# Two fused feed-forward layers behind a pooled attention on one core: a different byte offset for each token tile's streams, and 32 bytes for the second layer's weights

## The chip, the cores and the metric

One core of one Trainium2 chip runs the whole program. The metric is the device time of one execution in microseconds (us), the median of the runs shown; lower is better.

## The reference

The input x has 12,480 tokens of 128 channels. A pooled attention with 32 inducing rows comes first, and then two feed-forward layers of width 2048, each without a bias:

```python
h = mab(I, x); x = mab(x, h)              # softmax attention, scale 1/sqrt(128)
h = x @ w_in;  g = maximum(0.01 * h, h);  x = g @ w_out       # first layer
h = x @ w_in2; g = h / (1 + exp(-1.702 * h)); x = g @ w_out2  # second layer
```

## The kernel before

The tokens are cut into 25 token tiles: tiles 0 to 22 have 512 tokens, tiles 23 and 24 have 352. After a prologue that loads x, pools it and converts the weights (which arrive in a wider format), all work is a list of steps `(l, t, f)`: layer l, tile t, and one of NF = 16 blocks of 128 hidden units. The program is written out in that order by hand, so every engine's queue has the order of the code.

- `ffn_in` (L774 for the first layer, L778 to L780 for the second) multiplies a block of the input matrix with the tile's tokens into a PSUM bank `h_ps`. In the first layer this is one matmul, of `hw` (the pooled rows times the input matrix) with `at`, the attention weights of the tile. In the second it is three, because both operands are split into an upper and a lower part: `w2h` with `x2h`, `w2l` with `x2h`, `w2h` with `x2l`.
- `ffn_act` applies the nonlinearity on ScalarE (L788; L794 and L795) and writes the upper part `ghi`; VectorE writes the lower part `glo` (L789; L796).
- `ffn_out` (L806 to L808) adds three matmuls into the bank `acc`, of the output matrix `v1` or `v2` with `ghi`, `ghi` and `glo`. It runs LOOK = 3 steps behind `ffn_in`. The last block of a first-layer tile adds a matmul of `lin` with `at` (L810).

A step of the first layer so has four matmuls and one of the second has six. In each, the *stationary* operand is a 128x128 block of a weight matrix, which its own LDWEIGHTS brings in; the *stream* is the token side (`at`, `x2h`, `x2l`, `ghi`, `glo`), 512 or 352 columns of 4 bytes in each partition. All are of the type float32r.

The streams lie in the pool `main`: three buffers of `at`, five each of `ghi` and `glo`, two each of `x2h` and `x2l`, 2048 bytes per partition each. `at` of tiles 2 to 24 is filled by four DMAs of 64 KB on SyncE's queue (`stack`, L662), set ten steps before the tile's first step; `x2h` and `x2l` are filled by `halves` (ScalarE, and VectorE at L515), ten steps before the tile's first step in the second layer.

In the program's address map every weight block of both layers (`hw`, `v1`, `lin`, `w2h`, `w2l`, `v2`) begins 416 bytes past a multiple of 512, and every stream 480 bytes past one. The tiles named `gap` and `gap2` hold nothing; they push the tiles behind them to these positions. Since all sizes of these operands are multiples of 512 bytes, each stream begins 64 bytes behind its stationary operand, counted modulo 512. Below, this difference is called the *relation* of a matmul. One other float32r matmul has another relation: `linear_product` (L732) streams 256 columns of `v1` (at 416) against `hwT` (at 480), relation 448.

Of the kernel before, what the change touches and what calls it, by code (L numbers as in the profile page):

```python
# [10 lines left out]
F32 = mybir.dt.float32  # L11
F32R = mybir.dt.float32r
# [6 lines left out]
P = 128  # L19
LOOK = 3  # L20
# [37 lines left out]
def kernel(  # L58
# [14 lines left out]
    m = inducing.shape[0]  # L73
    DFF = moe_w_in.shape[1]
    NF = DFF // P
    TOK = TC * P
    NT = 2 + (N - 2 * TC * ENDS) // TOK
    assert N == 2 * TC * ENDS + (NT - 2) * TOK
    ch = [P] * (NT - 2) + [ENDS] * 2
    tok = [TC * k for k in ch]  # L80

    col = [TC * ENDS + TOK * t for t in range(NT - 2)] + [0, N - TC * ENDS]
    SCALE = 1.0 / math.sqrt(C)
    NQ = P // m
    NB = TOK // B
    PSUM = bass.MemoryType.PSUM

    const = ctx.enter_context(tc.tile_pool(name="const", bufs=1))
    slots = ctx.enter_context(tc.tile_pool(name="slots", bufs=1))
    wts = ctx.enter_context(tc.tile_pool(name="wts", bufs=1))  # L90
# [4 lines left out]

    mid = (NT - 2) * TOK
    x_mid = x[0, :mid].rearrange("(p j) c -> p j c", p=P)
# [77 lines left out]

    def matrix_in(src, name, tag):

        hi, lo = (wts.tile([P, DFF], F32R, name=f"{name}{h}", tag=f"{tag}{h}") for h in "hl")
        parts = []
        for o in range(0, DFF, CW):  # L180
            c = slice(o, o + CW)
            parts.append((src[:, c].bitcast(U32), hi[:, c], lo[:, c]))
        return (hi, lo), parts

    def matrix_out(src, name):

        w = wts.tile([P, NF, 2, C], F32R, name=name)
        parts = []
# [4 lines left out]
        return w, parts  # L193


    w1 = wts.tile([P, DFF], F32, name="w1", tag="wh")
    w1_parts = [
        (moe_w_in[:, o : o + CW].bitcast(U32), w1[:, o : o + CW], None)
        for o in range(0, DFF, CW)
# [62 lines left out]
    l = xnp.tile([P, NP], F32, name="l")  # L262
# [7 lines left out]
    def slot(t, dtype, name):  # L270
        return slots.tile([P, TOK], dtype, tag=f"slot{t}", name=f"{name}{t}")

# [231 lines left out]
    main = ctx.enter_context(tc.tile_pool(name="main", bufs=2))  # L504
    ps_a = ctx.enter_context(tc.tile_pool(name="ps_a", bufs=2, space=PSUM))


    main.tile([P, 112], F32, tag="gap", name="gap", bufs=1)

    def halves(src, name, pool=const, tag=None):  # L510
        shape = list(src.shape)
        hi = pool.tile(shape, F32R, name=f"{name}h", tag=f"{tag or name}h")
        lo = pool.tile(shape, F32R, name=f"{name}l", tag=f"{tag or name}l")
        nc.scalar.activation(out=hi, in_=src, func=AF.Copy)
        nc.vector.tensor_tensor(out=lo, in0=src, in1=hi.bitcast(F32), op=ALU.subtract)  # L515
        return hi, lo


    at_t = {}

    def weights_tile():


        return main.tile([P, TOK], F32R, tag="at", name="at", bufs=3)

    def token_tile(t, rest):

        st = {}
        n = ch[t]
        bc = lambda v: v.rearrange("p (j u) -> p j u", u=1).to_broadcast([n, TC, m])  # L530
        tiny = lambda name: main.tile([P, TC], F32, tag=name, name=name, bufs=2)[:n]

        def s0():
            ps = ps_h.tile([P, 512], F32, tag="h", name="s2_ps")
            for k in range(TC):
                nc.tensor.matmul(
                    ps[:n, k * m : (k + 1) * m], xT[t][:, k * n : (k + 1) * n],
                    hT[:, 0, :], start=True, stop=True,
                )
            st["ps"] = ps  # L540

        def s0b():
            ps = st["ps"]
            sv = ps[:n, : TC * m].rearrange("p (j k) -> p j k", j=TC)
            mxt = tiny("nmx")
            nc.vector.tensor_reduce(out=mxt, in_=sv, axis=AX.X, op=ALU.max)
            a = main.tile([P, TC, m], F32, tag="na", name="na", bufs=2)[:n]
            nc.vector.tensor_tensor(out=a, in0=sv, in1=bc(mxt), op=ALU.subtract)
            nc.scalar.activation(out=a, in_=a, func=AF.Exp, scale=SCALE)
            st["a"] = a  # L550

        def s1():
            a = st["a"]
            sst = tiny("nsum")
            nc.vector.tensor_reduce(out=sst, in_=a, axis=AX.X, op=ALU.add)
            nc.vector.tensor_scalar_add(sst, sst, EPS)
            nc.vector.reciprocal(sst, sst)
            nc.vector.tensor_tensor(out=a, in0=a, in1=bc(sst), op=ALU.mult)

        def s2():  # L560
            a = st["a"]
            rows = main.tile([P, TC, NQ, m], F32R, tag="rows", name="rows", bufs=2)[:n]
            dup = lambda v: v.rearrange("p j (u k) -> p j u k", u=1).to_broadcast(
                [n, TC, 2, m]
            )
            hi, lo = rows[:, :, 0:NQ:2, :], rows[:, :, 1:NQ:2, :]
            nc.vector.tensor_copy(hi, dup(a))
            rest.tensor_tensor(out=lo, in0=dup(a), in1=hi.bitcast(F32), op=ALU.subtract)
            st["rows"] = rows

        def s3():
            ps = ps_h.tile([P, 512], F32, tag="h", name="rows_ps")
            for k in range(TC):
                nc.tensor.transpose(
                    ps[:, k * n : (k + 1) * n],
                    st["rows"][:, k].rearrange("p q k -> p (q k)").bitcast(F32),
                    ident[:n, :n],
                )
            at_t[t] = weights_tile()[:, : tok[t]]
            nc.scalar.activation(out=at_t[t], in_=ps[:, : tok[t]], func=AF.Copy)  # L580

        return [s0, s0b, s1, s2, s3]

    NG = (NT - 2 + NQ - 1) // NQ
    hl = [None] * NG
# [71 lines left out]

    def stack(t):
        g, q = divmod(t - 2, NQ)
        a = weights_tile()[:, : tok[t]]  # L660
        for k in range(NQ):
            nc.sync.dma_start(  # L662
                out=a[k * m : (k + 1) * m, :].bitcast(F32),
                in_=hl[g][k % 2][q * m : (q + 1) * m, : tok[t]],
            )
        at_t[t] = a
# [62 lines left out]
    def linear_product(b):  # L729
        for k in range(4):  # L730
# [3 lines left out]
                v1[:, f].rearrange("p h c -> p (h c)"),  # L734
                start=(f == 0), stop=(f == NF - 1),
            )
# [25 lines left out]
    x2_t = {}  # L762
    x2h_t = {}
# [18 lines left out]

    def ffn_act(l, t, f):
        o = h_t.pop((l, t, f))
        hi = main.tile([P, TOK], F32R, tag="ghi", name="ghi", bufs=LOOK + 2)[:, : tok[t]]
        lo = main.tile([P, TOK], F32R, tag="glo", name="glo", bufs=LOOK + 2)[:, : tok[t]]
        if l == 0:
            nc.scalar.activation(out=hi, in_=o, func=AF.Relu)  # L788
            nc.vector.scalar_tensor_tensor(  # L789
                out=lo, in0=o, scalar=0.0, in1=hi.bitcast(F32), op0=ALU.max, op1=ALU.subtract  # L790
            )
        else:
            g = main.tile([P, TOK], F32, tag="g", name="g")[:, : tok[t]]
            nc.scalar.activation(out=g, in_=o, func=AF.Silu, scale=BETA)  # L794
            nc.scalar.activation(out=hi, in_=g, func=AF.Copy)  # L795
            nc.vector.tensor_tensor(out=lo, in0=g, in1=hi.bitcast(F32), op=ALU.subtract)  # L796
        g_t[l, t, f] = (hi, lo)

    def ffn_out(l, t, f):
# [4 lines left out]
        v = v1 if l == 0 else late["v2"]  # L804
        end = l == 1 and f == NF - 1
        nc.tensor.matmul(o, v[:, f, 0, :], hi, start=(f == 0), stop=False)  # L806
        nc.tensor.matmul(o, v[:, f, 1, :], hi, start=False, stop=False)  # L807
        nc.tensor.matmul(o, v[:, f, 0, :], lo, start=False, stop=end)  # L808
        if l == 0 and f == NF - 1:
            nc.tensor.matmul(o, lin, at_t.pop(t), start=False, stop=True)  # L810
# [23 lines left out]

    steps = [(l, t, f) for l in range(2) for t in range(NT) for f in range(NF)]
    steps[: 2 * NF] = [(0, t, 4 * b + f) for b in range(NF // 4) for t in (0, 1) for f in range(4)]

# [7 lines left out]
    first = token_tile(0, nc.vector)  # L845
# [41 lines left out]
    for t in range(2, NT):  # L887
        at((t - 1) * NF + (10 if t == 2 else 6), stack, t)

    def late_matrix(make, src, name, args, first):  # L890
# [8 lines left out]
        at(first, begin)  # L899

    late_matrix(matrix_in, moe2_w_in, "w2", ["w"], 60)
    late_matrix(matrix_out, moe2_w_out, "v2", [], 160)

    gaps = []

    def split_x2(t):

        if not gaps:
            gaps.append(main.tile([P, 96], F32, tag="gap2", name="gap2", bufs=1))
        x2h_t[t] = halves(x2_t.pop(t), "x2", main)  # L910

    for t in range(NT):
        at(NT * NF + (t - 1) * NF + 6, split_x2, t)

    for n in range(len(steps) + LOOK):
        if n < len(steps):
            ffn_in(*steps[n])
            ffn_act(*steps[n])
        if n >= LOOK:
            l, t, f = steps[n - LOOK]  # L920
            ffn_out(l, t, f)
            if f == NF - 1:
                ffn_end(l, t)
        for stage in extra.pop(n, []):
            stage()
# [39 lines left out]
```

## Time and profile before

| | |
|---|---|
| median of 2 runs | 964.12 us (963.95 to 964.28) |
| the profiled execution: span from first to last instruction | 962.6 us |
| TensorE (PE) busy | 953.7 us, 99% of the span |
| weight loads (PEld) busy | 779.5 us, 81% |
| ScalarE (ACT) busy | 783.0 us, 81% |
| VectorE (DVE) busy | 631.5 us, 66% |
| GpSimd (POOL) busy | 52.8 us, 5% |

The span stands 1.5 us under the median of the runs; that much lies around it. A matmul's own duration is longer than the distance to the next one's start, since matmuls overlap in the pipeline. What a matmul costs is therefore read as the distance between starts, and the busy share of PE says only that it has no gaps.

### The profile page before, as it was taken

The numbers are of one execution on the slowest core, as the hardware profiler recorded it, in microseconds if no ns is written. First come the engines' busy times: TensorE is split into PE (matmuls) and PEld (weight loads), VectorE is DVE, ScalarE is ACT, GpSimd is POOL, SyncE is SP. The second block draws the span as 40 slices with busy tenths as digits, with TensorE's granted clock in tenths as the row PEclk, the third lists the DMA queues.
The fourth block names the chain that finished last, engine by engine and source line by source line (L and its number), as shares of the span: only waits on it lengthen the run. The fifth ranks groups of instructions, "written<-read, shape, count | busy, mean of one in ns | idle before, by whom it ended". The sixth has DMA issues, their size and how long they took to land.

```text
span 962.6 us, 13196 instructions
## 1 busy us (share of the span) xinstructions
PE 953.7 (99%) x4577; PEld 779.5 (81%) x4577; DVE 631.5 (66%) x1002; ACT 783.0 (81%) x1357; POOL 52.8 (5%) x64
## 2 busy tenths in 40 slices
PE   8999999999999999999999999999999999999998
PEld 6677787887878878898888888888888888888888
DVE  3897788878878777765555555555555555555554
ACT  6666777767767666689999999999999999999998
POOL 1330101102100010000000000000000000000000
PEclk9999999999999999999999999999999999999999
DMA  9302120021000000000000000000000000000000
GB/s 337 107 1 55 34 66 23 20 81 33 23 22 12 23 12 19 8 1 12 12 12 12 12 11 12 15 19 12 12 11 12 12 12 12 12 12 23 12 12 16
DMA packets 15334, 27.90 MB, mean 29 GB/s; under 512 B 2347, under 2 KB 6987, under 8 KB 15267
## 3 DMA queue, kind: packets, MB, share of 16 engines
q1 hardware_dynamic: 15123, 26.88, 9.0%
q8 instruction: 36, 0.59, 0.3%
q14 instruction: 31, 0.25, 0.1%
q10 hardware_dynamic: 144, 0.18, 0.1%
HBM read 14.79 MB, written 6.39 MB: 22 GB/s over the span
## 4 chain that ended last, share of the span: by engine, by line
PE 94%; DVE 3%; DMA 1%; ACT 1%; issue 0%; POOL 0%; SPq 0%; ACTq 0%; POOLq 0%
PE acc L806 18%; PE acc L808 18%; PE acc L807 18%; PE h_ps L778 9%; PE h_ps L780 9%; PE h_ps L779 9%; PE h_ps L774 9%; DVE glo L789 1%; DMA xn<-in_x_dram 1%; PE s_ps L609 1%; PE xT_ps L279 1%; PE acc L810 1%; PE pv_ps L348 0%; DVE v L158 0%; DVE v L153 0%
## 5 line engine op out<-in xcount | busy, mean ns | idle before, releaser
L796 DVE TENSOR_TENSOR glo<-g,ghi 128x512 fp32r<-128x512 f32 (+1 forms) x400 | 271.7, 679 | 236.8 <-ACT ghi L795 223.2
L788 ACT ACTIVATE ghi<-h_ps 128x512 fp32r<-128x512 f32 (+1 forms) x400 | 232.2, 587 | 97.8 <-PE h_ps L774 96.2
L806 PE MATMUL acc<-ghi,v 128*128 128x512 f32 (+1 forms) x800 | 309.8, 387 | 0.0
L789 DVE SCALAR_TENSOR_TENSOR glo<-h_ps,ghi 128x512 fp32r<-128x512 f32 (+1 forms) x400 | 264.4, 674 | 68.8 <-ACT ghi L788 63.8
L808 PE MATMUL acc<-glo,v 128*128 128x512 f32 (+1 forms) x800 | 309.2, 386 | 0.1
L807 PE MATMUL acc<-ghi,v 128*128 128x512 f32 (+1 forms) x800 | 307.5, 384 | 0.0
L794 ACT ACTIVATE g<-h_ps 128x512 f32<-128x512 f32 (+1 forms) x400 | 234.3, 586 | 33.7 <-PE h_ps L780 0.6
L795 ACT ACTIVATE ghi<-g 128x512 fp32r<-128x512 f32 (+1 forms) x400 | 248.4, 621 | 12.7
L808 PEld LDWEIGHTS acc<-glo,v 128*128 128x128 f32 x800 | 150.2, 188 | 32.2 <-DVE glo L789 0.6
L807 PEld LDWEIGHTS acc<-ghi,v 128*128 128x128 f32 x800 | 150.2, 188 | 30.5
L806 PEld LDWEIGHTS acc<-ghi,v 128*128 128x128 f32 x800 | 150.3, 188 | 28.6 <-issue 0.2
L774 PE MATMUL h_ps<-at,hw 128*128 128x512 f32 (+1 forms) x400 | 155.7, 390 | 0.0
L778 PE MATMUL h_ps<-x2h,w2h 128*128 128x512 f32 (+1 forms) x400 | 155.3, 388 | 0.0
L780 PE MATMUL h_ps<-x2l,w2h 128*128 128x512 f32 (+1 forms) x400 | 154.5, 386 | 0.0
L779 PE MATMUL h_ps<-x2h,w2l 128*128 128x512 f32 (+1 forms) x400 | 153.1, 383 | 0.0
L774 PEld LDWEIGHTS h_ps<-at,hw 128*128 128x128 f32 x400 | 75.1, 188 | 18.8 <-issue 3.8
L780 PEld LDWEIGHTS h_ps<-x2l,w2h 128*128 128x128 f32 x400 | 75.1, 188 | 16.2
L779 PEld LDWEIGHTS h_ps<-x2h,w2l 128*128 128x128 f32 x400 | 75.1, 188 | 15.5
L778 PEld LDWEIGHTS h_ps<-x2h,w2h 128*128 128x128 f32 x400 | 75.2, 188 | 13.8
L824 ACT ACTIVATE x<-acc 128x512 f32<-128x512 f32 (+1 forms) x25 | 14.7, 587 | 7.6 <-PE acc L810 7.6
L515 DVE TENSOR_TENSOR x2l<-x,x2h 128x512 fp32r<-128x512 f32 (+1 forms) x25 | 16.8, 672 | 0.0
L283 ACT ACTIVATE xT<-xT_ps 128x512 f32<-128x512 f32 (+1 forms) x25 | 12.7, 586 | 4.6 <-PE xT_ps L279 4.6
(111 smaller groups left out, 312.7 us busy)
## 6 DMA issues: line engine op xcount, KB each, us to landing
out_dram<-o_t SPq DMA_DIRECT2D x23, 256.0 KB, 2.0
xn<-in_x_dram SPq DMA_DIRECT2D x11, 512.0 KB, 9.3
raw<-in_moe_w_in_dram SPq DMA_DIRECT2D x8, 512.0 KB, 5.3
raw<-in_moe_w_out_dram SPq DMA_DIRECT2D x8, 512.0 KB, 4.8
at<-hlhi SPq DMA_DIRECT2D x42, 64.0 KB, 2.0
at<-hllo SPq DMA_DIRECT2D x42, 64.0 KB, 2.0
xn<-in_x_dram SPq DMA_DIRECT2D x1, 352.0 KB
xn<-in_x_dram SPq DMA_DIRECT2D x1, 256.0 KB, 12.4
```

The lines of the kernel that those rows point to most:

```text
L774: nc.tensor.matmul(o, hw[:, cols], at_t[t], start=True, stop=True)
L778: nc.tensor.matmul(o, wh[:, cols], hi, start=True, stop=False)
L779: nc.tensor.matmul(o, wl[:, cols], hi, start=False, stop=False)
L780: nc.tensor.matmul(o, wh[:, cols], lo, start=False, stop=True)
L788: nc.scalar.activation(out=hi, in_=o, func=AF.Relu)
L789: nc.vector.scalar_tensor_tensor(out=lo, in0=o, scalar=0.0, in1=hi.bitcast(F32), op0=ALU.max, op1=ALU.subtract)
L794: nc.scalar.activation(out=g, in_=o, func=AF.Silu, scale=BETA)
L795: nc.scalar.activation(out=hi, in_=g, func=AF.Copy)
L796: nc.vector.tensor_tensor(out=lo, in0=g, in1=hi.bitcast(F32), op=ALU.subtract)
L806: nc.tensor.matmul(o, v[:, f, 0, :], hi, start=(f == 0), stop=False)
L807: nc.tensor.matmul(o, v[:, f, 1, :], hi, start=False, stop=False)
L808: nc.tensor.matmul(o, v[:, f, 0, :], lo, start=False, stop=end)
```

## The change

Each stream buffer gets 512 bytes of room (LINE = 128 elements), and a token tile lays its stream at an offset of its own in it. `place(l, t)` gives the offset in elements: 0 for the two tiles of 352 and for tile 0 (in the first layer tile 1 too, in the second tile 22 too); else 32, 64, ... 512 bytes for sixteen tiles in order, and then 4, 8, 16, 24 and 48 bytes for five more. In the first layer the list begins at tile 2, in the second at tile 1. The second layer's matrices `w2h`, `w2l` and, behind them, `v2` lie 32 bytes later, at 448; the gap is shortened by 32 bytes, so that a stream with offset 0 stays at 480. No instruction is added, taken away or moved in its queue. In the address map after the change, the relation of tile t is 32 + 32 t modulo 512 in both layers for tiles 2 to 16.

```
+    LINE = 128
+    SHIFT = 8
...
-        hi, lo = (wts.tile([P, DFF], F32R, name=f"{name}{h}", tag=f"{tag}{h}") for h in "hl")
+        hi = wts.tile([P, DFF + LINE], F32R, name=f"{name}h", tag=f"{tag}h")[:, SHIFT : SHIFT + DFF]
+        lo = wts.tile([P, DFF + SHIFT], F32R, name=f"{name}l", tag=f"{tag}l")[:, SHIFT:]
...
-    w1 = wts.tile([P, DFF], F32, name="w1", tag="wh")
+    w1 = wts.tile([P, DFF + LINE], F32, name="w1", tag="wh")[:, :DFF]
...
-    main.tile([P, 112], F32, tag="gap", name="gap", bufs=1)
+    main.tile([P, 104], F32, tag="gap", name="gap", bufs=1)
+
+    PLACES = [8 * k for k in range(1, 17)] + [1, 2, 4, 6, 12]
+
+    def place(l, t):
+        first = 2 if l == 0 else 1
+        return PLACES[t - first] if first <= t < first + len(PLACES) and t < NT - 2 else 0
+
+    def stream(name, bufs, l, t):
+        o = place(l, t)
+        return main.tile([P, TOK + LINE], F32R, tag=name, name=name, bufs=bufs)[:, o : o + tok[t]]
...
+    def halves(src, t):
+        hi = stream("x2h", 2, 1, t)
+        lo = stream("x2l", 2, 1, t)
...
+    def weights_tile(t):
+        return stream("at", 3, 0, t)
...
-        hi = main.tile([P, TOK], F32R, tag="ghi", name="ghi", bufs=LOOK + 2)[:, : tok[t]]
-        lo = main.tile([P, TOK], F32R, tag="glo", name="glo", bufs=LOOK + 2)[:, : tok[t]]
+        hi = stream("ghi", LOOK + 2, l, t)
+        lo = stream("glo", LOOK + 2, l, t)
```

## Rows read from the trace of the kernel before

**Rows 1.** The page: shares of the span by engine, and the chain that ended last.
```profile
PE 953.7 (99%) x4577; PEld 779.5 (81%) x4577; DVE 631.5 (66%) x1002; ACT 783.0 (81%) x1357; POOL 52.8 (5%) x64
...
PE 94%; DVE 3%; DMA 1%; ACT 1%; issue 0%; POOL 0%; SPq 0%; ACTq 0%; POOLq 0%
PE acc L806 18%; PE acc L808 18%; PE acc L807 18%; PE h_ps L778 9%; PE h_ps L780 9%; PE h_ps L779 9%; PE h_ps L774 9%; DVE glo L789 1%; DMA xn<-in_x_dram 1%; PE s_ps L609 1%; PE xT_ps L279 1%; PE acc L810 1%; PE pv_ps L348 0%; DVE v L158 0%; DVE v L153 0%
```

**Rows 2.** Busy time by stretch: first layer, second layer, 352-token tiles of the second.
```profile
core 0: us, PE busy (x) PEld busy (x) DVE busy (x) ACT busy (x) POOL busy (x), PEclk, DMA share, GB/s
305.00:340.00 35.00, 35.00 (x155) 28.71 (x154) 26.86 (x41) 23.57 (x40) 0.00 (x0) 1.00 0.10 23
500.00:600.00 100.00, 100.00 (x438) 82.06 (x437) 55.20 (x82) 90.79 (x150) 0.00 (x0) 1.00 0.03 11
926.00:956.00 30.00, 30.00 (x185) 29.60 (x184) 17.50 (x34) 28.47 (x63) 0.00 (x0) 1.00 0.05 16
```

**Rows 3.** One line's instructions, L774, 305 to 340 us: durations, first and last start.
```profile
L774 PE MATMUL h_ps<-at,hw x38: 388/392/394, 305.3 to 339.7; 128*128 128x512 f32 x38
```

**Rows 4.** The same view of L778, 500 to 600 us, then from 926 us on.
```profile
L778 PEld LDWEIGHTS h_ps<-x2h,w2h x73: 188/188/188, 500.0 to 598.9; 128*128 128x128 f32 x73
L778 PE MATMUL h_ps<-x2h,w2h x73: 394/394/394, 500.2 to 599.1; 128*128 128x512 f32 x73
...
L778 PE MATMUL h_ps<-x2h,w2h x32: 321/321/324, 926.0 to 956.4; 128*128 128x352 f32 x32
```

**Rows 5.** Timeline of PE near 59 and 37 us (start, us, what); one matmul's duration.
```profile
59.34 0.63 PE L732 MATMUL lin_ps<-v,hwT 128*128 128x256 f32 x4
...
L732 PE MATMUL lin_ps<-v,hwT x16: 280/281/682, 59.3 to 73.6; 128*128 128x256 f32 x16
...
36.90 0.60 PE L118 MATMUL idle_ps<-idle 128*128 128x256 bf16 x4
...
L118 PE MATMUL idle_ps<-idle x19: 272/421/421, 1.2 to 5.7; 128*128 128x256 bf16 x19
```

**Rows 6.** Groups of instructions by line, 500 to 600 us, then 305 to 340 us.
```profile
L796 DVE TENSOR_TENSOR glo<-g,ghi 128x512 fp32r<-128x512 f32 x74 | 51.3, 693 | 45.3 <-ACT ghi L795 42.6 <-PE h_ps L780 2.3
L795 ACT ACTIVATE ghi<-g 128x512 fp32r<-128x512 f32 x73 | 46.1, 632 | 2.3
L794 ACT ACTIVATE g<-h_ps 128x512 f32<-128x512 f32 x73 | 43.6, 597 | 6.8
...
L789 DVE SCALAR_TENSOR_TENSOR glo<-h_ps,ghi 128x512 fp32r<-128x512 f32 x39 | 26.7, 690 | 8.4 <-ACT ghi L788 8.4
L788 ACT ACTIVATE ghi<-h_ps 128x512 fp32r<-128x512 f32 x38 | 22.7, 599 | 10.9 <-PE h_ps L774 10.8
```

**Rows 7.** Line L662, the DMAs that fill `at`: issues, and time to landing.
```profile
L662 SPq DMA_DIRECT2D at<-hlhi x46: 507/578/1926, 75.5 to 389.0; - x46
L662 SPq DMA_DIRECT2D at<-hllo x46: 507/589/1612, 76.2 to 389.6; - x46
...
DMA to landing us min/median/max: 1.8/2.0/4.8
```

More of the change, by code (lines that the diff above doesn't have):

```diff
@@ L505 @@
     ps_a = ctx.enter_context(tc.tile_pool(name="ps_a", bufs=2, space=PSUM))
-    main.tile([P, 112], F32, tag="gap", name="gap", bufs=1)
[L510 to L513, printed above, removed]
+    main.tile([P, 104], F32, tag="gap", name="gap", bufs=1)
[9 more added lines that the diff above has]
+        lo = stream("x2l", 2, 1, t)
         nc.scalar.activation(out=hi, in_=src, func=AF.Copy)
@@ L519 @@
     at_t = {}
-    def weights_tile():
-        return main.tile([P, TOK], F32R, tag="at", name="at", bufs=3)
+    def weights_tile(t):
+        return stream("at", 3, 0, t)
     def token_tile(t, rest):
@@ L578, in s3 @@
                 )
-            at_t[t] = weights_tile()[:, : tok[t]]
+            at_t[t] = weights_tile(t)
             nc.scalar.activation(out=at_t[t], in_=ps[:, : tok[t]], func=AF.Copy)
@@ L659, in stack @@
         g, q = divmod(t - 2, NQ)
-        a = weights_tile()[:, : tok[t]]
+        a = weights_tile(t)
         for k in range(NQ):
@@ L909, in split_x2 @@
             gaps.append(main.tile([P, 96], F32, tag="gap2", name="gap2", bufs=1))
-        x2h_t[t] = halves(x2_t.pop(t), "x2", main)
+        x2h_t[t] = halves(x2_t.pop(t), t)
     for t in range(NT):
```

## The prediction

> **What bounds the kernel now.** I read the page's shares and the chain that ended last first: TensorE is busy 99% of the span, and 94% of the chain is its matmuls, nearly all of them the seven lines of the two layers [rows 1]. So time can come or go only where one matmul follows the next. [...]
>
> [...] In the second layer 73 starts of L778 lie between 500.2 and 599.1 us: 72 steps of six matmuls, 432 in 98.9 us, or 228.9 ns each [rows 4]. In the first layer 38 starts of L774 lie between 305.3 and 339.7 us: 37 steps of four matmuls and two of L810, 150 in 34.4 us, or 229 ns [rows 3]. The two layers differ in what ACT and DVE do meanwhile and in which buffers they read, and the distance is the same. The 352-column tiles: 31 steps of six from 926.0 to 956.4 us, of which nine matmuls (three steps of the tile before) are still 512 wide; (30.4 - 9 x 0.2289) / 177 gives 160.1 ns [rows 4]. Between the two widths a column costs (228.9 - 160.1) / 160 = 0.43 ns.
>
> **The change part by part.** Nothing is removed, added or moved in a queue; only addresses change. Their prices:
>
> *Streams at another relation.* The streams of 21 tiles in each layer move: 21 x 65 matmuls in the first (16 blocks of four and L810) and 21 x 96 in the second, 3,381 in all. In the second layer tiles 0 and 22 keep their stream but the weights move by 32 bytes: 192 more, which makes 3,573 of 512 columns, and 192 of 352. Each 32-byte step of the relation then holds about one tile of each layer, 64 + 96 = 160 matmuls or 36.6 us; no relation has much weight by itself. What does a matmul cost at another relation? The trace has just one of the same type: L732, 256 columns at relation 448. Four of them take 0.63 us from the first start to the last end; less the duration of one, 0.28, three distances are 0.35 us, 117 ns each [rows 5]. The line through 160.1 and 228.9 gives 228.9 - 256 x 0.43 = 118.8 ns for 256 columns at relation 64. The other relation is within 2 ns, and not on the dear side. This is the row nearest to the edit, so I cost the new relations at 0 ns. It is one relation of sixteen, so the ends stay open. Above: the load of the stationary operand takes 188 ns [rows 4] and lies wholly beside the matmul before it; where it could not, a matmul would cost up to 229 + 188. [...]
>
> *The 32 bytes of the second layer's weights.* They change absolute places, not the work; the first layer's blocks at 416 and the second's cost the same 229 ns today only because they lie alike, so no row prices this edit by itself. It is in the bounds above, at 0.
>
> *Starts off the 32-byte grid.* Five places (4, 8, 16, 24 and 48 bytes), 160 matmuls each, 800 in all. No row has such a start. A price that fits the columns: at most one 32-byte step more to read, eight columns of 0.43 ns or 3.4 ns a matmul, 2.8 us; at least nothing. I take 1 us. The upper end is another rival, below.
>
> *The engines that write the streams.* ACT and DVE write `ghi`, `glo`, `x2h` and `x2l` at the new places. A step lasts 6 x 228.9 = 1,373 ns in the second layer and 916 ns in the first. ACT needs 597 + 632 = 1,229 ns in the second and 599 in the first, DVE 693 and 690 [rows 6]. The cover is 144 ns of ACT in each second-layer step, less some 40 for its share of the split of x2 (one 632 ns instruction in 16 steps): about 100 ns, or 16% on L795. It hides a slower write up to there. I cost it at nothing; if the cover is gone, a write of twice the duration makes a step 597 + 1,264 = 1,861 ns and a tile of 16 steps 7.8 us longer.
>
> *The DMAs into `at`.* Four issues of some 0.58 us and a landing of 2.0 us, at most 4.8 [rows 7], against ten steps x 0.916 = 9.2 us of lead. They are covered unless a landing takes over twice the worst one seen.
>
> The sum: 964.12 + 0 + 0 + 1 + 0 + 0 = **965 us**. By the profiled execution it is 962.6 + 1 in the span and 1.5 us around it.
>
> [...]
>
> **The rivals.**
>
> *The load meets the stream (slower).* Stationary operand and stream are read from the same memory at the same time, and where both start at the same place modulo 512 the load might be held up. For it: the load runs for 188 of the 229 ns [rows 4], so both read together most of the time, and no row shows float32r at relation 0. Against it: L732 at 448, and that the load starts with its matmul but moves along its 512 bytes while the stream runs through 2048, so that they pass each other at any relation. Relation 0 is tile 15 of both layers, 160 matmuls; held up by the whole load, 160 x 0.188 = 30 us: **994 us**. It decides (over 2%) from 19.3 us, which is 121 ns a matmul at this one relation, or 5.4 ns if every moved matmul pays.
>
> *Off-grid starts read at half rate (slower).* If a stream that begins at an odd element needs two reads for a pair, the tile of 4 bytes runs at up to twice 229 ns: 160 x 0.2 = 32 us at most, **996 us**. No row speaks for it; none excludes it, since every stream today begins on 32 bytes.
>
> [...]
>
> *The change doesn't do what it says.* If the placement rounded the offsets away, nothing would change: **964 us**.
>
> **How the numbers follow.** A measurement of this kernel can tell about 2% from no change. Forecast, 965 us: 0.57. The load that meets the stream: 0.20, of which 0.16 passes 2%. Half rate: 0.09, of which 0.08 passes. Dear place: 0.09, of which 0.04 passes (a bit more than half of the moved matmuls freed). No effect of the edit: 0.05. So faster 0.04, same 0.57 + 0.04 + 0.01 + 0.05 + 0.05 = 0.72, slower 0.24. The range takes in the two slower prices and some two thirds of the faster rival's 15 us: 953 to 998 us. About 0.07 is left out below and 0.1 above, where several relations would pay.
>
> **What would show it.** The profile after should give 229 ns from start to start of L774 and L778 in every tile, 188 ns for a load, and no gap in PE. [...] Durations of L788, L795, L789 and L796 that rise in some tiles would show the writers. The prediction is wrong if distances depend on the relation over a run of tiles: a single row at 448 carries that step, and it is the weakest one.

## The result and the profile after

The changed kernel takes 976.67 us (median of 2 runs, 976.38 to 976.96) against 964.12 us: a ratio of 1.0129, 95% interval 1.01 to 1.0159. It is slower by 12.6 us. The profiled execution has a span of 975.2 us, 12.6 us over that of before.

On the page after, the busy shares of the engines and the first two lines of the chain answer to [rows 1]:

```profile
PE 966.4 (99%) x4577; PEld 780.0 (80%) x4577; DVE 632.3 (65%) x1002; ACT 783.4 (80%) x1357; POOL 52.7 (5%) x64
...
PE 94%; DVE 3%; DMA 1%; ACT 1%; issue 0%; POOL 0%; SPq 0%; ACTq 0%; POOLq 0%
PE acc L818 18%; PE acc L817 18%; PE acc L816 18%; PE h_ps L790 9%; PE h_ps L788 9%; PE h_ps L789 9%; PE h_ps L784 9%; DVE glo L799 1%; DMA xn<-in_x_dram 1%; PE s_ps L619 1%; PE acc L820 1%; PE xT_ps L282 1%; PE pv_ps L351 0%; DVE v L160 0%; DVE v L155 0%
```

The whole difference is PE's: 966.4 against 953.7 us busy, with the same 4,577 matmuls and the same chain. All other engines are busy for as long as before, within 1 us. PE has no new gaps; its matmuls follow one another more slowly.

They do so tile by tile. The next rows are of the second layer's first matmul (L788, which was L778), one row for one tile: 16 instructions with their durations (min/median/max) and the first and last start. They are tiles 1, 4, 7, 15 and 17, at relations 64, 160, 256, 0 and 36; the last row is of 352-column tiles, at relation 32. They answer to [rows 4].

```profile
L788 PE MATMUL h_ps<-x2h,w2h x16: 387/388/399, 448.3 to 468.9; 128*128 128x512 f32 x16
...
L788 PE MATMUL h_ps<-x2h,w2h x16: 391/397/400, 515.1 to 536.2; 128*128 128x512 f32 x16
...
L788 PE MATMUL h_ps<-x2h,w2h x16: 389/389/396, 582.3 to 602.8; 128*128 128x512 f32 x16
...
L788 PE MATMUL h_ps<-x2h,w2h x16: 389/389/396, 760.6 to 781.1; 128*128 128x512 f32 x16
...
L788 PE MATMUL h_ps<-x2h,w2h x16: 392/397/400, 804.8 to 826.0; 128*128 128x512 f32 x16
...
L788 PE MATMUL h_ps<-x2h,w2h x24: 322/323/323, 938.6 to 961.3; 128*128 128x352 f32 x24
```

Fifteen steps of six matmuls are 90 distances: 20.6 us is 229 ns, 21.1 us is 234, 20.5 us (twice) is 228 and 21.2 us is 236. The last row: 23 steps of six, nine matmuls of them from a tile of 512; (22.7 - 9 x 0.233) / 129 is 160 ns, as before. The duration that the trace gives a matmul moves with the distance, which allows a finer reading below: 391.3 ns as the mean of 394, 388 and 392 [rows 3, 4] at 228.9 ns, so distance is duration less 162 to 163 ns.

From the starts of L788 in each tile (the fourth to the sixteenth, 72 distances, so that with LOOK = 3 no matmul of the tile before lies between) comes the table, by relation:

```
relation  32-byte grid: 0 32 64 96 128 160 192 224 | 256 288 320 352 384 416 448 480
ns        226.8 233.3 229.1 233.5 233.3 234.2 233.3 233.3 | 226.8 233.3 229.1 233.5 233.3 234.2 233.3 233.3
off the grid: 36 -> 234.9, 40 -> 233.3, 48 -> 230.0, 56 -> 230.0, 80 -> 231.1
```

The distance repeats with 256 bytes of relation. Before, every matmul was at 64, which with 320 is the second cheapest place on the 32-byte grid: only 0 and 256 are cheaper. First-layer tiles, against weights at 416, have the same distances on the grid within 0.2 ns by the seventh to the sixteenth start of L784 (the matmuls of L619 come before), except at 128 and 384: 232.4.

The writers did not change. Groups by line of the dear tile 4, 515 to 536 us; they answer to [rows 6], with 693, 597 and 632 ns:

```profile
L806 DVE TENSOR_TENSOR glo<-g,ghi 128x512 fp32r<-128x512 f32 x16 | 11.1, 693 | 10.2 <-ACT ghi L805 10.1
L804 ACT ACTIVATE g<-h_ps 128x512 f32<-128x512 f32 x16 | 9.5, 596 | 2.0
L805 ACT ACTIVATE ghi<-g 128x512 fp32r<-128x512 f32 x15 | 9.5, 632 | 0.5
```

### The profile page after: what moved, and what is told of

It is laid out like the page before. It is cut to its first block, busy times and chain, and to the rows that moved or that the text cites. A ratio compares the mean times of both kernels' runs of the same rounds, so it can differ in the third digit from the quotient of the medians.

```text
span 975.2 us, 13196 instructions
## 1 busy us (share of the span) xinstructions
PE 966.4 (99%) x4577; PEld 780.0 (80%) x4577; DVE 632.3 (65%) x1002; ACT 783.4 (80%) x1357; POOL 52.7 (5%) x64
## 4 chain that ended last, share of the span: by engine, by line
PE 94%; DVE 3%; DMA 1%; ACT 1%; issue 0%; POOL 0%; SPq 0%; ACTq 0%; POOLq 0%
PE acc L818 18%; PE acc L817 18%; PE acc L816 18%; PE h_ps L790 9%; PE h_ps L788 9%; PE h_ps L789 9%; PE h_ps L784 9%; DVE glo L799 1%; DMA xn<-in_x_dram 1%; PE s_ps L619 1%; PE acc L820 1%; PE xT_ps L282 1%; PE pv_ps L351 0%; DVE v L160 0%; DVE v L155 0%
## 5 line engine op out<-in xcount | busy, mean ns | idle before, releaser
L818 PE MATMUL acc<-glo,v 128*128 128x512 f32 (+1 forms) x800 | 311.0, 389 | 0.1
L817 PE MATMUL acc<-ghi,v 128*128 128x512 f32 (+1 forms) x800 | 310.9, 389 | 0.0
L816 PE MATMUL acc<-ghi,v 128*128 128x512 f32 (+1 forms) x800 | 310.8, 388 | 0.0
L805 ACT ACTIVATE ghi<-g 128x512 fp32r<-128x512 f32 (+1 forms) x400 | 248.9, 622 | 12.7
L818 PEld LDWEIGHTS acc<-glo,v 128*128 128x128 f32 x800 | 150.3, 188 | 33.5 <-DVE glo L799 0.5
L817 PEld LDWEIGHTS acc<-ghi,v 128*128 128x128 f32 x800 | 150.2, 188 | 32.5
L816 PEld LDWEIGHTS acc<-ghi,v 128*128 128x128 f32 x800 | 150.2, 188 | 32.3 <-issue 0.2
L784 PE MATMUL h_ps<-at,hw 128*128 128x512 f32 (+1 forms) x400 | 156.5, 392 | 0.0
L790 PE MATMUL h_ps<-x2l,w2h 128*128 128x512 f32 (+1 forms) x400 | 155.4, 388 | 0.0
L788 PE MATMUL h_ps<-x2h,w2h 128*128 128x512 f32 (+1 forms) x400 | 155.4, 388 | 0.0
L789 PE MATMUL h_ps<-x2h,w2l 128*128 128x512 f32 (+1 forms) x400 | 155.3, 388 | 0.0
L784 PEld LDWEIGHTS h_ps<-at,hw 128*128 128x128 f32 x400 | 75.0, 188 | 19.9 <-issue 3.8
L788 PEld LDWEIGHTS h_ps<-x2h,w2h 128*128 128x128 f32 x400 | 75.1, 188 | 16.5
L790 PEld LDWEIGHTS h_ps<-x2l,w2h 128*128 128x128 f32 x400 | 75.1, 188 | 16.4
L789 PEld LDWEIGHTS h_ps<-x2h,w2l 128*128 128x128 f32 x400 | 75.1, 188 | 16.3
L834 ACT ACTIVATE x<-acc 128x512 f32<-128x512 f32 (+1 forms) x25 | 14.7, 586 | 8.0 <-PE acc L820 8.0
## 6 DMA issues: line engine op xcount, KB each, us to landing
xn<-in_x_dram SPq DMA_DIRECT2D x1, 256.0 KB, 11.7
```

The source lines that it names most:

```text
L784: nc.tensor.matmul(o, hw[:, cols], at_t[t], start=True, stop=True)
L788: nc.tensor.matmul(o, wh[:, cols], hi, start=True, stop=False)
L789: nc.tensor.matmul(o, wl[:, cols], hi, start=False, stop=False)
L790: nc.tensor.matmul(o, wh[:, cols], lo, start=False, stop=True)
```

## The experiments

The theory after the result: where a stream begins against the stationary operands, modulo 256 bytes, sets the distance of 512-column matmuls. The rivals: that places differ between tiles; that starts off the 32-byte grid cost; that the stream's own place counts. Medians below are each compared with runs of the kernel before on the same chip.

**One half of the change alone: the weights' 32 bytes.** Edit, on the changed kernel:

```
     def place(l, t):
         first = 2 if l == 0 else 1
-        return PLACES[t - first] if first <= t < first + len(PLACES) and t < NT - 2 else 0
+        return 0
```

Expected: 

> The second layer's weights 32 bytes later, all streams at offset 0: every second-layer matmul at relation 32, every first-layer one at 64. Theory (the relation to the stationary operand sets the distance; the tiles at relation 32 after the change cost 233.0 ns against 228.9): 23 x 96 = 2,208 matmuls x 4.1 ns = 9 us more, 973 us, with 229 ns in the first layer and 233 in the second. Rival (starting places that differ between tiles, or starts off the 32-byte grid, are what costs): 964 us and 229 ns in both layers.

Measured: 973.97 us against 964.59, ratio 1.0098 (1.0082 to 1.0113). L788 of the second layer, 500 to 600 us, and L784 of the first, 305 to 340 us:

```profile
L788 PE MATMUL h_ps<-x2h,w2h x72: 396/396/397, 499.9 to 599.3; 128*128 128x512 f32 x72
...
L784 PE MATMUL h_ps<-at,hw x38: 388/392/394, 305.0 to 339.3; 128*128 128x512 f32 x38
```

71 x 6 matmuls in 99.4 us are 233.3 ns in the second layer; the first has the durations of before [rows 3]. Nothing differs between tiles here and nothing is off the grid: a shift of 32 bytes costs 4.4 ns a matmul, and the rival falls.

**The other half: the offsets alone.** Edit, on the changed kernel: `SHIFT = 0`, and the gap back at 112.

Expected: 

> The tiles' offsets without the 32 bytes of the second layer's weights. Theory of the relation: the second layer's tiles now meet the relations 96 to 64 that the first layer's met, sum of their excess over 228.9 ns 74 ns over 21 tiles, times 65 + 96 matmuls: 11.9 us, 976 us; the second-layer tile at 416 becomes cheap (228 ns) in place of the one at 448. Rival of the absolute place of the stream: each second-layer tile keeps the distance that it had after the change (cheap at 192 and 448).

Measured: 976.71 us against 964.59, ratio 1.0126 (1.0109 to 1.0143). By the starts of each second-layer tile, the cheap ones (226.7 ns) are now those at 160 and at 416, relations 256 and 0 to the weights at 416; with the weights at 448 they were those at 192 and 448. The cheap place goes with the weights, so the stream's own place does not make it. The halves cost 9.4 and 12.1 us and together 12.6: they do not add, since the offsets sweep all relations wherever the weights lie.

**Relation 0 throughout.** Edit, on the kernel before:

```
-    main.tile([P, 112], F32, tag="gap", name="gap", bufs=1)
+    main.tile([P, 96], F32, tag="gap", name="gap", bufs=1)
```

Expected: 

> The kernel before with a gap of 96 in place of 112 elements: every stream and every stationary operand at 416, relation 0. Theory: 227.5 ns in every tile of 512, 3,703 matmuls x 1.4 ns = 5 us less than before, 959 us. Rival (the load meets the stream where both start at the same place, as predicted): over 229 ns, slower than 964 us. Rival of the changing places: 964 us.

Measured: 956.64 us against 964.59, ratio 0.9918 (0.9903 to 0.9933): faster than both kernels. L778, L779 and L780, 500 to 600 us:

```profile
L778 PE MATMUL h_ps<-x2h,w2h x74: 389/389/389, 500.1 to 599.4; 128*128 128x512 f32 x74
...
L779 PE MATMUL h_ps<-x2h,w2l x74: 389/389/389, 500.3 to 599.6; 128*128 128x512 f32 x74
...
L780 PE MATMUL h_ps<-x2l,w2h x74: 389/389/389, 500.5 to 599.8; 128*128 128x512 f32 x74
```

73 x 6 matmuls in 99.3 us are 226.7 ns, and each line has one duration where before there were three in turn. The place that the first rival of the prediction held to be the dear one is the cheapest.

**The dearest relation throughout.** The same edit with 136 in place of 112.

Expected: 

> The kernel before with a gap of 136 elements: every stream at 64, every stationary operand at 416, relation 160, the dearest one on the 32-byte grid in the sweeps (234.0 ns in the run with the offsets alone). Theory of the relation: 234.0 ns in every 512-column tile, 3,703 x 5.1 ns = 19 us over the kernel before, 983 us; the 352-column tiles at 160 ns as in every run so far. Rival (the dear distances come from neighbouring tiles that differ): under 970 us.

Measured: 983.61 us against 964.55, ratio 1.0192 (1.0175 to 1.0209). L778, 500 to 600 us, and the 352-column tiles, from 946 us:

```profile
L778 PE MATMUL h_ps<-x2h,w2h x72: 392/397/400, 499.8 to 599.6; 128*128 128x512 f32 x72
...
L778 PE MATMUL h_ps<-x2h,w2h x31: 321/321/327, 946.6 to 975.9; 128*128 128x352 f32 x31
```

71 x 6 in 99.8 us are 234.3 ns; the 352-column tiles have (29.3 - 6 x 0.234) / 174 = 160 ns. So the sweep's distance for a relation holds when all tiles have it, and the narrow tiles hardly depend on it: by their starts, 160.0 ns at 64, 160.2 at 160, and 161.1 in the second layer with relation 0.

**Half of the tiles 256 bytes on.** Edit, on the kernel with the offsets alone: gap 96, and `place` returns `64 * (t % 2)`.

Expected: 

> Relation 0, with the streams of every odd tile 256 bytes later. If what counts is the relation modulo 256 and tiles may differ freely, 227 ns in all tiles and 956.6 us, as with relation 0. If places that differ from tile to tile cost by themselves, some ns in the steps in which two tiles interleave (3 of 16): about 960 us. If the relation counts modulo 512, odd tiles are dear: 965 us or more.

Measured: 957.12 us against 964.35, ratio 0.9922 (0.9907 to 0.9937), as with relation 0. L788, 500 to 600 us:

```profile
L788 PE MATMUL h_ps<-x2h,w2h x73: 389/389/390, 500.7 to 598.7; 128*128 128x512 f32 x73
```

72 x 6 in 98.0 us are 226.9 ns: here tiles that lie 256 bytes apart alternate at no cost, and 256 bytes is the period.

**Starts off the grid, first by 4 bytes.** Edit: relation 0 in both layers, but in the second `SHIFT = 1`, `place` returns `l`, and `v2` begins one element into a longer tile too.

Expected: 

> Relation 0, but in the second layer every stream and every stationary operand begins 4 bytes later, at 420, off the 32-byte grid. If the relation alone counts: 227 ns in both layers, 956.6 us as with relation 0. If a start off the grid costs by itself, as the tiles at 484 seem to say (236.7 ns at relation 68 against 229.8 at 64): up to 7 ns on 2,208 matmuls, up to 972 us.

Measured: 981.93 us against 964.55, ratio 1.0177 (1.0161 to 1.0192). L790, 500 to 600 us, and its 352-column tiles from 944 us:

```profile
L790 PE MATMUL h_ps<-x2h,w2h x70: 401/401/401, 500.4 to 598.9; 128*128 128x512 f32 x70
...
L790 PE MATMUL h_ps<-x2h,w2h x31: 322/329/331, 943.9 to 974.0; 128*128 128x352 f32 x31
```

69 x 6 in 98.5 us are 237.9 ns at relation 0, 11 ns over the cheap one and more than I expected. Here even the narrow tiles pay: (30.1 - 6 x 0.238) / 174 = 165 ns. So the relation isn't all; this start, 4 bytes off the grid, costs by itself. Both operands are moved here; the fine sweep below has the stream alone at 420, relation 4, and there it costs 236.5 ns.

**Off the grid by 16 bytes.** The same with 4 elements in place of 1.

Expected: 

> Relation 0; in the second layer every stream and stationary operand begins 16 bytes later, at 432: on a 16-byte grid, off the 32-byte one. With 4 bytes the same edit cost 10.7 ns a matmul. If the place within 16 bytes is what cost there, 227 ns in both layers and 957 us. If the place within 32 bytes is, up to 238 ns in the second layer and 982 us.

Measured: 971.07 us against 964.35, ratio 1.0067 (1.0052 to 1.0082). L790, 500 to 600 us:

```profile
L790 PE MATMUL h_ps<-x2h,w2h x72: 395/396/397, 500.5 to 599.9; 128*128 128x512 f32 x72
```

71 x 6 in 99.4 us are 233.3 ns. Neither of the two answers: this start, at 432, costs 6.6 ns at relation 0, less than the 11 ns of the one at 420.

**A fine sweep around 0.** Edit, on the kernel with the offsets alone: gap 80, `PLACES = [6 + k for k in range(21)]`, both layers from tile 1, all others at relation 0.

Expected: 

> Tiles 1 to 21 at relations -40 to 40 bytes in steps of 4, tile 11 at 0, all others at 0; no shift of the second layer's weights. Theory: the cheapest tile is that at 0 (227.5 ns), those at -32 and 32 cost 233 ns; the shape between is open. If it falls smoothly to 0, starts at 4 and 8 bytes cost under 229 ns; if only equal places are cheap, all but tile 11 cost 231 to 237 ns and the time is some 973 us.

Measured: 976.23 us (one run). L788 of tiles 10, 11 and 12, at -4, 0 and 4 bytes:

```profile
L788 PE MATMUL h_ps<-x2h,w2h x16: 387/387/390, 648.6 to 669.1; 128*128 128x512 f32 x16
...
L788 PE MATMUL h_ps<-x2h,w2h x16: 389/389/395, 670.5 to 690.9; 128*128 128x512 f32 x16
...
L788 PE MATMUL h_ps<-x2h,w2h x16: 392/398/399, 692.3 to 713.5; 128*128 128x512 f32 x16
```

By the starts of the fourth to the sixteenth: -4 is as cheap as 0 (226.7 and 226.8 ns), 4 costs 236.5. It is no valley. The places that are 4 bytes past a multiple of 16 cost 233 to 237 ns, all five; those 12 bytes past one 227 to 230, all five; those 8 bytes past one 230 to 234, all six. Neither of my shapes holds. No place is cheaper than 0 by more than 0.1 ns, but in this layer -20, -4 and 28 are as cheap (226.7, 226.7 and 226.8 ns): not every start off the grid costs, and 0 is not the only cheap relation.

**Which operand?** Edit, on relation 0: the low matrix of the second layer alone begins 32 bytes later.

```
+        lo = wts.tile([P, DFF + 128], F32R, name=f"{name}l", tag=f"{tag}l")[:, 8 : 8 + DFF]
```

Expected: 

> Relation 0, and the second layer's low matrix alone 32 bytes later (448), everything else in place. Which operand counts? If it is the one loaded while a stream runs, that is the next matmul's: the distance from the first matmul of a second-layer step (whose stream runs while the low matrix is loaded) rises from 227.5 to about 233 ns and the other five stay; 368 x 5.6 ns = 2 us more than with relation 0, 961 us. If it is the matmul's own stationary operand, the second one rises in its place. If places of the written buffers count, nothing changes, since none moves.

Measured: 964.12 us against 964.59, ratio 0.9995 (0.9986 to 1.0005), so 7.5 us over relation 0 where I expected 2. Groups of PE by line, 500 to 600 us; a step runs L779, L780 (the product with the low matrix), L781, L807, L808, L809:

```profile
L779 PE MATMUL h_ps<-x2h,w2h 128*128 128x512 f32 x73 | 29.0, 397 | 0.0
L781 PE MATMUL h_ps<-x2l,w2h 128*128 128x512 f32 x73 | 28.8, 395 | 0.0
L808 PE MATMUL acc<-ghi,v 128*128 128x512 f32 x73 | 28.4, 389 | 0.0
L809 PE MATMUL acc<-glo,v 128*128 128x512 f32 x73 | 28.4, 389 | 0.0
L780 PE MATMUL h_ps<-x2h,w2l 128*128 128x512 f32 x73 | 28.4, 389 | 0.0
L807 PE MATMUL acc<-ghi,v 128*128 128x512 f32 x72 | 28.3, 393 | 0.0
```

Relation 0 has 389 ns in all of them. The matmul that runs while the moved matrix is loaded pays most (8 ns), its own product nothing to speak of; that part is as the theory has it. But the next two, whose operands have not moved, pay 6 and 4. No buffer that is written in the second layer moved, so writers aren't needed for the effect.

**Half of that load.** Edit, on the kernel above: `nc.tensor.matmul(o[: P // 2], wl[:, f * P : f * P + P // 2], hi, ...)`.

Expected: 

> As the kernel whose low matrix alone lies 32 bytes later, but the product with the low matrix has 64 of its 128 columns: it leaves out the low part for the upper half of each block of hidden units, so that the load at the other relation is half as long while the streams stay 512 columns. If the reading of the load beside the stream makes the cost, the first matmul of a step falls from 235.0 ns to about 231 and the time from 964.1 us to about 960. If the place of the matrix costs in another way (as the matmul's own operand, or by time that has gone by), 235 ns and 964 us stay.

Measured: 966.4 us against 964.55, ratio 1.0018 (1.0009 to 1.0027). Groups of PE by line, 500 to 600 us; a step runs L779, L780 (the halved product), L783, L809, L810, L811:

```profile
L811 PE MATMUL acc<-glo,v 128*128 128x512 f32 x73 | 28.7, 393 | 0.0
L783 PE MATMUL h_ps<-x2l,w2h 128*128 128x512 f32 x72 | 28.6, 398 | 0.0
L779 PE MATMUL h_ps<-x2h,w2h 128*128 128x512 f32 x73 | 28.5, 391 | 0.0
L810 PE MATMUL acc<-ghi,v 128*128 128x512 f32 x72 | 28.4, 395 | 0.0
L780 PE MATMUL h_ps<-x2h,w2l 128*64 128x512 f32 x72 | 28.3, 393 | 0.0
L809 PE MATMUL acc<-ghi,v 128*128 128x512 f32 x72 | 28.0, 389 | 0.0
```

The first matmul fell to a duration of 391 ns, 228 ns of distance where I expected 231, but other lines rose and the time with them. That needed a control.

**Its control, at relation 0.** The same edit with the low matrix in its old place.

Expected: 

> The control of the half load: all at relation 0, and the product with the low matrix has 64 of 128 columns (it leaves out the low part for the upper half of each block of hidden units). If a load of another length by itself disturbs the matmuls that follow, distances over 230 ns appear in lines whose operands have not moved, and the time lies between 960 and 967 us. If not, 227 ns throughout and 956.6 us, and the half load's rises came from the moved matrix.

Measured: 963.6 us against 964.35, ratio 0.9992 (0.9983 to 1.0001). Groups of PE by line, 500 to 600 us; a step runs L778, L779 (the halved product), L782, L808, L809, L810. The last row is the halved load:

```profile
L779 PE MATMUL h_ps<-x2h,w2l 128*64 128x512 f32 x73 | 29.0, 397 | 0.0
L808 PE MATMUL acc<-ghi,v 128*128 128x512 f32 x73 | 28.8, 395 | 0.0
L810 PE MATMUL acc<-glo,v 128*128 128x512 f32 x73 | 28.4, 389 | 0.0
L782 PE MATMUL h_ps<-x2l,w2h 128*128 128x512 f32 x73 | 28.4, 389 | 0.0
L778 PE MATMUL h_ps<-x2h,w2h 128*128 128x512 f32 x73 | 28.3, 388 | 0.0
L809 PE MATMUL acc<-ghi,v 128*128 128x512 f32 x72 | 28.3, 393 | 0.0
...
L779 PEld LDWEIGHTS h_ps<-x2h,w2l x73: 134/134/134, 499.9 to 599.3; 128*64 128x64 f32 x73
```

At relation 0 everywhere, a shorter load costs 7 us by itself, and in the same figure: 397, 389, 395, 393 ns over four matmuls, as behind the moved matrix. Here it begins one matmul later, at the halved product, and with both edits together (398, 389, 395, 393) one later still. In these three runs the figure is worth some 20 ns of distance over four matmuls. Moving the matrix raises the first matmul by 8 ns with the whole load (389 to 397) and by 3 with half of it (388 to 391), which fits a cost of the load beside the stream. But a matmul of 397 ns appears at relation 0 too, where nothing was moved; the half load can't part what the moved load costs from what any break in the sequence costs.

**One stream moved.** Edit, on relation 0 by the helper `stream`: `o = 8 if name == "x2l" else 0`.

Expected: 

> Relation 0, and the stream of the third matmul of a second-layer step alone 32 bytes later. Theory (a stream pays while the next load runs beside it, and disturbs the following ones): this matmul's distance rises from 227 to about 235 ns, those of the next three by some 1, 6 and 4 ns, as they did behind the moved low matrix, and 964 us. Rival (the matmul's own operands alone): 233 ns in this line, 227 in all others, 368 x 6.5 ns: 959 us.

Measured: 965.46 us against 964.35, ratio 1.0012 (1.0003 to 1.0022). The theory's time (964) is near and the rival's (959) is not. But the pattern is not the one that I gave: in the order of the step (L788, L789, L790 with the moved stream, L816, L817, L818) the mean durations are 391, 390, 395, 391, 395 and 394 ns, so all six lines pay, the moved one 6 ns. Groups of PE by line, and the durations of L790 (min/median/max), 500 to 600 us:

```profile
L817 PE MATMUL acc<-ghi,v 128*128 128x512 f32 x73 | 28.8, 395 | 0.0
L818 PE MATMUL acc<-glo,v 128*128 128x512 f32 x73 | 28.8, 394 | 0.0
L816 PE MATMUL acc<-ghi,v 128*128 128x512 f32 x73 | 28.5, 391 | 0.0
L790 PE MATMUL h_ps<-x2l,w2h 128*128 128x512 f32 x72 | 28.4, 395 | 0.0
L788 PE MATMUL h_ps<-x2h,w2h 128*128 128x512 f32 x72 | 28.2, 391 | 0.0
L789 PE MATMUL h_ps<-x2h,w2l 128*128 128x512 f32 x72 | 28.1, 390 | 0.0
...
L790 PE MATMUL h_ps<-x2l,w2h x72: 392/393/399, 500.8 to 599.1; 128*128 128x512 f32 x72
```

The means hide that the pattern repeats only after three steps: L790 has 392, 399 and 393 ns in turn.

## Why the prediction was right, and which of its steps were off

No change beyond 2% was forecast, and 976.67 us is 1.3% more and lies in the range of 953 to 998; but 965 us was 11.7 us short, and the measured change is clear of noise. Its main step was wrong: distances depend on the relation over a run of tiles, which the prediction itself had named as the sign that it is wrong. That the time stayed under 2% all the same was luck: the moved matmuls pay 12.6 us / 3,573 = 3.5 ns on average, while the prediction had put this price at nothing and its bounds at up to 188 ns. By its steps:

- *PE bounds, and only distances can change.* Right: the difference of the spans, 12.6 us, is PE's busy time (12.7 us).
- *Streams at another relation cost 0 ns.* This step failed. On the 32-byte grid the second layer's table has a mean of 3.2 ns over 228.9, 50.8 ns over sixteen relations; times 160 matmuls each this is 8.1 us. The row that carried the step had 256 columns. It could not show the price, since narrow matmuls hardly pay on the grid: four matmuls of that line take the same time, 0.63 or 0.64 us, at relation 0 (gap 96), at 352 (gap 136) and at 64 (fine sweep). One group of four from the timeline of each of these kernels:

```profile
58.77 0.63 PE L732 MATMUL lin_ps<-v,hwT 128*128 128x256 f32 x4
```

```profile
69.49 0.63 PE L732 MATMUL lin_ps<-v,hwT 128*128 128x256 f32 x4
```

```profile
59.92 0.63 PE L742 MATMUL lin_ps<-v,hwT 128*128 128x256 f32 x4
```

  The line through 352 and 512 columns then joined a matmul that hardly depends on the relation to one that does. The agreement at 256 was no evidence about 512.
- *The 32 bytes of the weights cost 0.* Off: by itself 9.4 us. In the whole change they count through the relations, and by themselves only in tiles 0 and 22, 192 x 4.4 ns = 0.8 us.
- *Starts off the grid, 1 us.* Mis-sized: the five places cost 14.7 ns together over 228.9 in the second layer's table, times 160 is 2.4 us, within the 0 to 2.8 us that I had given. The upper end was an estimate, eight columns of 0.43 ns [rows 4]; measured, the five places pay 1.1 to 6.0 ns each. These three terms make 11.3 of 12.6 us; of the rest, 0.5 us is the first layer's dearer fine places (22.3 ns together over the 229.1 of its tiles at 64 and 320, by their starts from the fifth on, in place of 14.7, 64 matmuls each), and in the profiled executions the first layer begins 0.6 us later (44.6 against 44.0 us). With both operands 16 bytes off at relation 0, a start costs 6.6 ns.
- *The writers and the DMAs into `at` stay covered.* Right for the writers (693, 596, 632 ns in the dear tile); the chain names DMAs and waits no more than before, so no DMA was late either.
- *The load meets the stream at relation 0.* The place was the opposite: 0 is cheapest, and most of the other relations pay some 4 to 5 ns, the spread form for which I had given 5.4 ns as the point that passes 2%. The mean stayed under it. That the two pass each other at any relation was my estimate, from their 512 and 2048 bytes and the load's 188 of 229 ns [rows 4]. Whether the load beside the stream is the mechanism is not settled (below).
- *Half rate off the grid.* Refuted: the worst is 11 ns (237.9 against 226.7), not 200. *The dear place*, the faster rival of the chances and of the range: no run shows the 15 us that the range takes for it; the most that the runs gave is 8.0 us, with relation 0 (956.64 against 964.59), and the cheap places go with the weights' place (160 and 416 against weights at 416, 192 and 448 against weights at 448). *No effect of the edit*: refuted (976.67 us).
- *How low the distance went.* No relation on the grid came under 226.7 ns, so relation 0 gives back 2.2 ns of the 228.9. With one loaded matrix moved by 32 bytes and nothing else, the matmul beside its load takes 8 ns more (397 for 389) and the kernel 7.5 us more; the runs don't show what is waited for.

What stays open is how the memory makes these differences: why a period of 256 bytes, why in the fine sweep a start 12 bytes past a multiple of 16 is cheap (227 to 230 ns) and one 4 bytes past dear (233 to 237), why 352 columns hardly pay on the grid (160.0 to 161.1), and why a break is paid over four matmuls or more (397, 389, 395, 393 ns of duration). That the load read beside the stream is the cause fits the moved matrix and its half, but a shortened load at relation 0 gave the same figure with nothing moved, and two operands moved alone gave patterns that the theory didn't foresee, so it isn't settled.

## What to carry to other kernels

In these kernels, whose float32r matmuls of 512 columns run without gaps, the place of the streamed operand against the loaded one was worth some per cent of the distance (226.7 to 234.3 ns on the 32-byte grid). Both on that grid at a difference of 0 or 256 bytes was the cheapest here; for another width or type, read the distance between starts. A row with another width was no stand-in for the price of an address (256 columns took 0.63 or 0.64 us at three relations), even if it fits on a line. And one operand out of line cost more than its share: one matrix of six loads 7.5 us, where the whole second layer at relation 32 costs 2,208 x 6.6 ns = 14.6 us over relation 0. Two of the three matmuls that follow paid too (395 and 393 ns for 389).

## What the runs showed that I had not expected

- At relation 0, 512 columns cost 226.7 ns with a single duration; at 64, 228.9 with three durations in turn (394, 388, 392); elsewhere on the grid up to 234.3.
- The same relation 0 with all operands 4 bytes off the grid costs 237.9 ns, with 16 bytes 233.3.
- One moved weight matrix of six loads in a step costs 7.5 us, and a load of 64 in place of 128 columns, which is less work (134 against 188 ns), costs 7 us.
